# Both pieces of a common slot and all transposes of an ordinary slot at one place between the products, scatters made independent, routing constants issued later

## The chip, the core and the metric

The kernel runs on one core of a Trainium2 chip. The metric is the device time of one execution in microseconds (us); the median of the runs shown is what counts. The engines are PE (TensorE, matrix products and transposes; its weight loads are listed as PEld), DVE (VectorE), ACT (ScalarE), POOL (GpSimd) and SP (SyncE, which only issues transfers). PE's clock has two levels in this case, 2.4 GHz (granted clock 1.00) and 1.2 GHz (0.50).

## The reference, cut to what matters

```python
# attention: B, H, S, D = 4, 8, 576, 64
scores = where(causal, -1e9, q @ k.T / sqrt(D))
local = softmax(scores) @ v
q_p = where(q > 0, q, exp(q) - 1) + 1
mem_out = (q_p @ M_prev) / (q_p @ z_prev + 1e-6)
x = sigmoid(beta) * mem_out + (1 - sigmoid(beta)) * local   # 2304 rows of 512
# mixture of experts: E = 8, F = 1024, one expert a row
logits = x @ w_gate
e_idx = argmax(logits); gate_w = softmax(logits)[e_idx]
eom = sigmoid(x @ w_output_gate)
for e in range(8):
    h = maximum(x[e_idx == e] @ w1[e], 0)
    out[e_idx == e] = gate_w * eom[:, e] * (h @ w2[e])
```

Which expert takes which row is known only at run time. Inputs and result are float32.

## The kernel before

The first part, to about 220 us, is attention. Its instructions stand in an order written out by hand: the string `ORDER` (L50 to L108) names jobs, and each is recorded when its name comes up. Letters tell the kind: `SS` scores on PE, `M` mask and row maximum on DVE, `E` the exponential on ACT, `T` transposes on PE, `V` copies of them out of PSUM, `P` products with v, `C` and `R` the split of q and k into a high part (ACT or DVE) and a low part (POOL, `lo` at L460), `F0` to `F2` the feature map, `TS` small copies of sums on POOL. Before the first job `constants()` (L193) is recorded: three loads and sixteen small POOL instructions that make the tables for the routing (`upper`, `pidx`, `sidx`, `edesc`, `cnt`, `less`, `back`, `tokv`). They are first read by the rank and routing jobs (`RK`, `RT`), which stand far down the string. Right behind them POOL has the last low part of the first tile (L472, `first_low`).

The second part is the mixture of experts. The rows are put into 17 ordinary slots of 128 rows (`NMAIN`), each for one expert. A slot `s` goes through `gather` (POOL, an indirect transfer of its rows), `stage_x` (four transposes on PE into `px`, L1376; two copies on ACT; the low part `xl` on POOL), `gemm1` (first product, 24 matrix products of 512 columns into `h`, L1405, then a rectifier on ACT, L1418), `stage_h` (eight transposes into `hp`, L1431; four copies on ACT; two low parts on POOL), `gemm2` (second product, 24 more into `py`, L1405; scaled on ACT, L1443) and `scatter` (POOL, an indirect transfer to the result). Operands are split into a high and a low part, three terms to a product.

Left-over rows of several experts share common slots: four quarters of 32 rows, then two halves of 64. The weights of such a slot come in 24 transfers of 1 MB (`wide_load`, issued by ACT, four or two instructions each) into two buffers used in turn, and each transfer is used up by one piece on PE (`unit`, L1586): for the quarters four column groups of 32 side by side, for the halves two of 64. Two pieces belong to each ordinary slot from 2 to 13 (`plan[s, 0]`, `plan[s, 1]`), sixteen of quarters in slots 2 to 9 and eight of halves in slots 10 to 13. `refill` issues the load for the buffer that a piece has just freed. A piece waits for its transfer by a semaphore (`T.wait_ge`, L1568).

In the loop (L1640) PE's program for slot `s` is, in this order: `gemm1` of slot s+1 (in four slots with the transposes of a common slot in its middle), the transposes of `stage_x` for slot s+2, the first piece, the first half of `gemm2` of slot s, the transposes of `stage_h` for slot s+1, the second half of `gemm2`, the second piece. The middle comes from the argument `mid`:

```python
i = point(s, 0)
refill(s, 0)
gemm2(s, lambda: (group_rows() if s == 0 else None, stage_h(s + 1)))
i = point(s, 1) or i
refill(s, 1)
```

The scatters all write the tensor `out`. Only those of the last two slots are told to be independent (group `"rows"`); each of the others waits until the one before has landed.

Of the kernel before, what the change touches and what calls it, by code (L numbers as in the profile page):

```python
# [23 lines left out]
NT = B * S  # L24
# [10 lines left out]
NMAIN = 17  # L35
# [20 lines left out]
C3:DVE F12 P1_0_0 E2_1_0 V1_4_1:DVE T2_0 load4 E1_3_0 E1_3_1 V2_0:DVE SS2_2 R3 M2_2_0 M2_2_1 O0_256:ACT O1_0:ACT SS2_3 T2_1 T1_3_1 load_v3 E2_2_0  # L56
V2_1:ACT M2_3_0 V1_3_1:ACT TS1_0 E2_3_0 SS2_4 T1_3_0 V1_3_0:ACT M2_3_1 MW1 F13 F04 E2_2_1 T2_2_0 T2_3_0 TS1_1 M2_4_0 P1_256_0 C4:DVE E2_3_1 F22 MC1
V2_2_0:ACT SS3_1 M3_0_0 V2_3_0:ACT P1_256_1 T2_2_1 M3_1_0 M2_4_1 E2_4 V2_2_1:ACT E3_0_0 load5 F23 O1_256:DVE M3_0_1 T2_3_1 TS2_0 load6 E3_0_1 E3_1_0
# [74 lines left out]
def attn_moe(ctx: ExitStack, tc: tile.TileContext, qk, vd, mz, mt, rz, beta, wgo, w1, w2, out):  # L133
# [59 lines left out]
    def constants():  # L193
        SY.dma_start(gt, beta.partition_broadcast(P))
        SY.dma_start(wg, wgo)
        SY.dma_start(rzt, rz)
        G.affine_select(upper, ones, pattern=[[1, P]], compare_op=ALU.is_gt, fill=0.0, base=0, channel_multiplier=-1)
        G.iota(pidx, pattern=[[1, P]], base=0, channel_multiplier=0, allow_small_or_imprecise_dtypes=True)
# [777 lines left out]
    job("gates", "ACT", 300, 2.0, gates, start=3300)  # L976
    job("gates2", "POOL", 200, 2.0, gates2, after=["gates"])
    job("wgz", "POOL", 300, 6.0, lambda: G.tensor_copy(wgz.rearrange("p n (j c) -> p n j c", j=2), rzt.rearrange("p n (j c) -> p n j c", j=2)[..., D:]) and None, start=4500)
    for g in range(NG):
# [50 lines left out]
    def star_out():  # L1030
        V.scalar_tensor_tensor(jc, stars, 65536.0, jc, op0=ALU.mult, op1=ALU.add)
# [325 lines left out]
    def star_y():  # L1357
        ze["y"] = mk.tile([P, F], F32, name="ye", tag="hl")[:, :DM]
        A.activation(ze["y"], ze["py"], AF.Copy, scale=st["e"]["g"])

    def star_out():
        y = ze.pop("y")
        G.indirect_dma_start(out=out, out_offset=bass.IndirectOffsetOnAxis(ap=rowe, axis=0), in_=y, in_offset=None, bounds_check=NT - 1, oob_is_err=False)

# [55 lines left out]

    def stage_h(s):
        h32 = st[s]["h"]
        hp = pa.tile([P, F], F32, name=f"hp{s}", tag="hp")
        hT = bq.tile([P, F], F32, name=f"hT{s}", tag="hT")
        if s == NMAIN - 1:
            own = cp.tile([P, 2, F], F32R, name="own", tag="w0")
            hh, hl = own[:, 0], own[:, 1]
        else:
            hh, hl = (mk.tile([P, F], F32R, name=f"h{n}{s}", tag=f"h{n}") for n in "hl")
        for f in range(8):  # L1430
            T.transpose(hp[:, f * P:(f + 1) * P], h32[:, f * P:(f + 1) * P], ident)  # L1431
        for n in range(2):
            z = slice(n * 512, (n + 1) * 512)
            A.copy(hT[:, z], hp[:, z])  # L1434
            A.copy(hh[:, z], hp[:, z])  # L1435
            G.tensor_tensor(hl[:, z], hT[:, z], f32(hh)[:, z], op=ALU.subtract)  # L1436
        st[s]["x2"] = hh, hl
# [8 lines left out]
    def finish(s):  # L1446
        for n in range(2):
# [4 lines left out]
            i = G.indirect_dma_start(out=out.rearrange("t (a d) -> (t a) d", a=2), out_offset=bass.IndirectOffsetOnAxis(ap=endi[:, n:n + 1], axis=0), in_=y, in_offset=None, bounds_check=2 * NT - 1, oob_is_err=False)  # L1452
            tc.add_to_no_dep_group("rows", i.ins)
            tc.declare_no_dep(i.ins, group="rows", reason="each slot and half writes its own part of the rows")
        done(s, sem_2)
        st.pop(s)

    def scatter(s):
        i = G.indirect_dma_start(out=out, out_offset=bass.IndirectOffsetOnAxis(ap=outi[:, s:s + 1] if s < NMAIN else fin["outf"][:, s - NMAIN:s - NMAIN + 1], axis=0), in_=st.pop(s)["y"], in_offset=None, bounds_check=NT - 1, oob_is_err=False)
        if s == NMAIN - 2:  # L1460
            tc.add_to_no_dep_group("rows", i.ins)

# [139 lines left out]
    def group_out_rows(kind):  # L1602
        y = mk.tile([P, DM], F32, name=f"yc{kind}", tag="y", bufs=2)
        A.activation(y, cst[kind, "y"], AF.Copy, scale=cst[kind, "g"])
        G.indirect_dma_start(out=out, out_offset=bass.IndirectOffsetOnAxis(ap=group_out[:, kind:kind + 1], axis=0), in_=y, in_offset=None, bounds_check=NT - 1, oob_is_err=False)

    loads = [(0, part, k) for part in range(2) for k in range(8)] + [(1, part, k) for part in range(2) for k in range(4)]
    plan = {}
# [3 lines left out]
    plan[3, "mid"] = lambda: group_turn(0)  # L1612
    plan[5, 1].append(lambda: group_relu(0))
    plan[7, "mid"] = lambda: group_h(0)
    plan[9, 1].append(lambda: group_out_rows(0))
    plan[11, "mid"] = lambda: group_turn(1)
    plan[11, 1].append(lambda: group_relu(1))
    plan[13, "mid"] = lambda: group_h(1)
# [21 lines left out]
    for s in range(NMAIN):  # L1640
        if 0 < s < NMAIN - 1:
            gemm1(s + 1, plan.get((s + 1, "mid")))
        if s + 2 < NMAIN:
            stage_x(s + 2)
            regs(s + 2)
        if s == 1:
            scatter(0)
# [5 lines left out]
        if s == NMAIN - 1:  # L1653
            finish(s)
            break
        i = point(s, 0)
        refill(s, 0)
        gemm2(s, lambda: (group_rows() if s == 0 else None, stage_h(s + 1)))
        i = point(s, 1) or i
        refill(s, 1)  # L1660
        if s == 13:
# [121 lines left out]
```

## Time and profile before

| | |
|---|---|
| runs shown | 478.33, 479.43 and 479.53 us, median 479.43 us |
| profiled execution | 479.24 us, of which the span of instructions is 477.4 us |
| PE | 465.1 us busy, 97% of the span |
| DVE, ACT, POOL | 283.8 us (59%), 262.6 us (55%), 266.0 us (56%) |
| transfers | 80.09 MB, 168 GB/s over the span |
| chain of work that ended last | 91% PE, 3% DVE, 2% POOL, 2% issue |

The profile is one execution. A busy engine is not one at its peak: PE counts as busy while a product drains, so what a change of kind costs it is seen from the starts of its instructions, one after the other, and not from its busy time.

### The profile page before, as it was taken

What the parts mean: (1) busy time and instruction counts of PE and PEld (TensorE: products, weight loads), DVE (VectorE), ACT (ScalarE), POOL (GpSimd) and SP (SyncE); (2) the same over time, 40 slices, a digit from 0 to 9 for tenths busy, and PEclk for the clock granted to TensorE, in tenths of its full rate; (3) what the DMA queues carried; (4) which work ended last, traced back from release to release, by engine and by line L of the source; (5) the groups of instructions that cost most, each with busy time, mean ns of one, the idle gap of its engine ahead of it and who ended that gap; (6) DMA issues with size and microseconds to landing.
All of it is one profiled execution on the core that took longest, in us unless ns stands there. A gap on an engine that the chain in (4) does not pass through costs nothing.

```text
span 477.4 us, 10482 instructions
## 1 busy us (share of the span) xinstructions
PE 465.1 (97%) x3315; PEld 347.9 (73%) x3315; DVE 283.8 (59%) x847; ACT 262.6 (55%) x621; POOL 266.0 (56%) x264
## 2 busy tenths in 40 slices
PE   7999999999999999998999999999999999999994
PEld 4877887877877787746787767767677676676884
DVE  4879898989889987888989807007089500000000
ACT  5889888888878776444543242352423422424241
POOL 8746584555734762453579664536448753443452
PEclk8999999999999999999999999999999999999998
DMA  7544065324131262243298979848699755450101
GB/s 236 186 152 139 23 206 176 136 80 171 56 123 49 85 182 103 67 154 90 66 386 291 336 268 302 288 159 263 224 319 321 273 160 185 141 185 30 36 22 40
DMA packets 34215, 80.09 MB, mean 168 GB/s; under 512 B 4820, under 2 KB 5352, under 8 KB 34154
## 3 DMA queue, kind: packets, MB, share of 16 engines
q1 hardware_dynamic: 17610, 44.05, 27.3%
q10 hardware_dynamic: 12688, 25.30, 15.6%
q0 software_dynamic: 3856, 9.98, 5.9%
q8 instruction: 32, 0.52, 0.5%
q14 instruction: 29, 0.24, 0.2%
HBM read 69.86 MB, written 9.97 MB: 167 GB/s over the span
## 4 chain that ended last, share of the span: by engine, by line
PE 91%; DVE 3%; POOL 2%; issue 2%; POOLq 0%; ACT 0%; DVEq 0%; ACTq 0%
PE h L1405 20%; PE py L1405 18%; PE po L675 10%; PE pt L640 8%; PE s L565 7%; PE me L731 4%; PE cy L1586 3%; PE ch L1586 3%; PE hp L1431 3%; PE sd L552 3%; PE pt L609 2%; PE px L1376 2%; PE pv L794 1%; PE pl L899 1%; PE pye L1130 1%
## 5 line engine op out<-in xcount | busy, mean ns | idle before, releaser
L1436 POOL TENSOR_TENSOR hl<-hT,hh 128x512 fp32r<-128x512 f32 x32 | 46.5, 1472 | 54.5 <-ACT hh L1435 54.5
L628 ACT ACTIVATE st<-st,nm 128x128 f32<-128x128 f32 (+3 forms) x128 | 71.4, 562 | 4.7 <-DVE nm L623 4.6
L1098 DVE CAST whi<-kept 128x1024 fp32r<-128x1024 f32 x32 | 30.0, 938 | 59.4 <-ACTq L1412 50.8
L623 DVE CUSTOM_DVE_ANT_0 st<-s,mask 128x128 f32<-128x128 f32 (+3 forms) x128 | 58.3, 483 | 9.7 <-PE s L565 5.6
L1405 PE MATMUL h<-whi,xh 128*128 (+1 forms) x136 | 55.8, 410 | 0.0
L460 POOL TENSOR_TENSOR lo<-qk,hi 128x1216 fp32r<-128x1216 f32 x15 | 42.1, 2808 | 24.4 <-ACT hi L456 19.0
L487 ACT COPY PT<-pt 128x512 f32<-128x512 f32 (+2 forms) x89 | 45.3, 523 | 15.9 <-PE pt L640 13.8
L1405 PE MATMUL h<-wlo,xh 128*128 (+1 forms) x136 | 53.2, 391 | 0.0
L1405 PE MATMUL h<-whi,xl 128*128 (+1 forms) x136 | 53.1, 391 | 0.0
L1405 PE MATMUL py<-whi,hh 128*128 (+1 forms) x128 | 53.0, 414 | 0.0
L1405 PE MATMUL py<-wlo,hh 128*128 (+1 forms) x128 | 50.2, 392 | 0.0
L1405 PE MATMUL py<-whi,hl 128*128 (+1 forms) x128 | 50.0, 391 | 0.0
L1101 DVE TENSOR_TENSOR wlo<-kept,whi 128x1024 fp32r<-128x1024 f32 x32 | 49.2, 1537 | 1.1
L675 PE MATMUL po<-PT,v 128*64 128x320 f32 (+4 forms) x480 | 49.1, 349 | 0.8 <-ACT oT_hT L487 0.4
L1418 ACT ACTIVATE h<-h 128x1024 f32<-128x1024 f32 x17 | 17.4, 1025 | 57.1 <-PE h L1405 57.1
L640 PE MATMUL pt<-ident,st 128*128 128x128 f32 x320 | 48.3, 282 | 0.0
L1434 ACT COPY hT<-hp 128x512 f32<-128x512 f32 x34 | 20.1, 591 | 49.6 <-PE hp L1431 49.6
L675 PEld LDWEIGHTS po<-PT,v 128*64 128x64 f32 x480 | 29.6, 137 | 17.7 <-issue 2.8
L1384 POOL TENSOR_TENSOR xl<-x,xh 128x512 fp32r<-128x512 f32 x17 | 23.0, 1356 | 32.7 <-ACT x L1383 31.2
L640 PEld LDWEIGHTS pt<-ident,st 128*128 128x128 f32 x320 | 35.8, 143 | 7.0 <-ACT PT L487 1.8
L1435 ACT CAST hh<-hp 128x512 fp32r<-128x512 f32 x32 | 19.1, 596 | 32.3 <-PE py L1405 32.3
L1405 PEld LDWEIGHTS h<-whi,xh 128*128 128x128 f32 x136 | 25.5, 188 | 15.2 <-ACT hh L1435 10.0
(337 smaller groups left out, 1026.3 us busy)
## 6 DMA issues: line engine op xcount, KB each, us to landing
kept<-in_w SPq DMA_DIRECT2D x32, 512.0 KB, 5.3
wide<-in_w ACTq DMA_DIRECT2D x64, 256.0 KB
qk<-in_qk SPq DMA_DIRECT2D x15, 640.0 KB, 4.6
wide<-in_w ACTq DMA_DIRECT2D x16, 512.0 KB
v<-in_vd SPq DMA_DIRECT2D x16, 320.0 KB, 4.3
xs<-xd SPq DMA_DIRECT2D x12, 256.0 KB, 2.2
star<-in_w SPq DMA_DIRECT2D x6, 512.0 KB, 5.2
mz<-in_mz SPq DMA_DIRECT2D x4, 324.0 KB
```

What stands on the lines that cost most here:

```text
L460: G.tensor_tensor(c["lo"][:, TQ:], c["raw"][:, TQ:], f32(c["hi"])[:, TQ:], op=ALU.subtract)
L487: (A.copy if e == "ACT" else V.tensor_copy)(dst(), src())
L565: T.matmul(c()["ss", q][j], l[r, lc], m[r, KC:KC + w], start=(a == 0), stop=(a == 2))
L623: V.tensor_tensor_reduce(st[:, :w], c()["ss", qt][j], mask[:, 512 - w:512], -SCALE, 3.0e38, ALU.add, ALU.min, negm()[:, i:i + 1])
L628: A.activation(st, st, AF.Exp, bias=c()["negm"][:, i:i + 1], scale=-1.0, accum_out=sums()[:, qt, 2 * p + j:2 * p + j + 1])
L640: T.transpose(pt[:, (m * k1 + i) * P:(m * k1 + i + 1) * P], st[:, i * P:(i + 1) * P], ident)
L675: T.matmul(po[64 * j:64 * j + 64, qs - q0:q1 - q0], vt[:, k, 64 * j:64 * j + 64], PT[:, j, k, qs:q1], start=(k == 0), stop=(k == kn - 1))
L1098: join((A.copy if eng is A else eng.tensor_copy)(whi[:, e % 2, c, :], raws[e, c]))
L1101: join(eng.tensor_tensor(wlo[:, e % 2, c, :], raws.pop((e, c)), f32(whi[:, e % 2, c, :]), op=ALU.subtract))
L1405: i = T.matmul(o[n % nh], l[:, z], m[:, n * 512 + part.start:n * 512 + part.stop], start=(c == 0 and k == 0 and n < nh), stop=(c == 3 and ...
L1436: G.tensor_tensor(hl[:, z], hT[:, z], f32(hh)[:, z], op=ALU.subtract)
L1586: i = apart(T.matmul(o[r], x[:, c * P + w * g:c * P + w * g + w], wt[:, g, z], start=first, stop=last, tile_position=(0, w * g)))
```

## The change

Five edits. In slots 2 to 13 (`paired`) both pieces are recorded one behind the other, right after `gemm1` of the next slot; the transposes of `stage_x` and those of `stage_h` follow them together, and `gemm2` runs through without a middle. The rectifier of a common slot (`group_relu`) moves from behind the second piece to behind the transposes of `stage_h` (`turned`). The first `refill` is now issued before the copies of `stage_x`, the second one after them and before the copies of `stage_h`. All scatters of the second part are declared independent of each other. The sixteen POOL instructions of the constants become a job `ranks` that stands behind `TS1_1` in `ORDER`.

```diff
-V2_1:ACT M2_3_0 V1_3_1:ACT TS1_0 ... T2_3_0 TS1_1 M2_4_0 P1_256_0 C4:DVE E2_3_1 F22 MC1
+V2_1:ACT M2_3_0 V1_3_1:ACT TS1_0 ... T2_3_0 TS1_1 ranks M2_4_0 P1_256_0 C4:DVE E2_3_1 F22 MC1
...
+    def ranking_constants():
         G.affine_select(upper, ones, pattern=[[1, P]], ...)
...
+    job("ranks", "POOL", 4000, 8.0, ranking_constants)
...
+    def own_rows(i):
+        tc.add_to_no_dep_group("rows", i.ins)
+        tc.declare_no_dep(i.ins, group="rows", reason="each slot, half and group writes its own rows or parts of them")
...
-    def stage_h(s):
+    def stage_h(s, turned=None):
...
             T.transpose(hp[:, f * P:(f + 1) * P], h32[:, f * P:(f + 1) * P], ident)
+        if turned:
+            turned()
...
     def scatter(s):
         i = G.indirect_dma_start(out=out, ...)
-        if s == NMAIN - 2:
-            tc.add_to_no_dep_group("rows", i.ins)
+        own_rows(i)
...
-    plan[5, 1].append(lambda: group_relu(0))
+    plan[5, "relu"] = lambda: group_relu(0)
...
-    plan[11, 1].append(lambda: group_relu(1))
+    plan[11, "relu"] = lambda: group_relu(1)
...
             gemm1(s + 1, plan.get((s + 1, "mid")))
+        paired = (s, 0) in plan
+        if paired:
+            i = point(s, 0)
+            refill(s, 0)
+            i = point(s, 1) or i
         if s + 2 < NMAIN:
             stage_x(s + 2)
             regs(s + 2)
+        if paired:
+            refill(s, 1)
+            stage_h(s + 1, plan.get((s, "relu")))
...
-        i = point(s, 0)
-        refill(s, 0)
-        gemm2(s, lambda: (group_rows() if s == 0 else None, stage_h(s + 1)))
-        i = point(s, 1) or i
-        refill(s, 1)
+        gemm2(s, None if paired else lambda: (group_rows() if s == 0 else None, stage_h(s + 1)))
```

What this does to PE's row of instructions is seen in slot 5 (`TENSOR_LOAD`, `REGISTER_ALU` and `ISA` set registers for the slots to come). On PE before, between the first product of slot 6 (`h`) and the second product of slot 5 (`py`), stood the transposes of slot 7's rows (`px`) and the first piece (`ch_0`):

```order
L1405 MATMUL h_4775<-wlo,xh_4677 128x512
L1376 MATMUL px_4806<-ident,xr_4636 128x128 x4
L1388 TENSOR_LOAD need
L1388 ISA x2
L1389 TENSOR_LOAD pari
L1389 ISA x2
L1586 MATMUL ch_0_4379<-wide_3964,cx 32x512 x4
L1400 REGISTER_ALU
L1405 ISA
L1405 MATMUL py_4846<-whi,hh_4730 128x512
```

The eight transposes of slot 6 (`hp`) parted the second product, and the second piece (`ch_1`) stood between its end and the first product of slot 7:

```order
L1405 MATMUL py_4846<-wlo,hh_4730 128x512
L1586 MATMUL ch_1_4380<-wide_4036,cx 32x512 x4
L1400 REGISTER_ALU
L1405 ISA
L1405 MATMUL h_4912<-whi,xh_4811 128x512
```

On PE after, both pieces, the four transposes and the eight stand in a row between the first product of slot 6 and the undivided second product of slot 5:

```order
L1413 MATMUL h_4775<-wlo,xh_4691 128x512
L1594 MATMUL ch_0_4348<-wide_3964,cx 32x512 x4
L1594 MATMUL ch_1_4349<-wide_4036,cx 32x512 x4
L1384 MATMUL px_4820<-ident,xr_4636 128x128 x4
L1396 TENSOR_LOAD need
L1396 ISA x2
L1397 TENSOR_LOAD pari
L1397 ISA x2
L1439 MATMUL hp_4853<-ident,h_6_4803 128x128 x8
L1408 REGISTER_ALU
L1413 ISA
L1413 MATMUL py_4876<-whi,hh_4721 128x512
```

So three visits to other work in a slot have become one, and the transposes of `hp` now come that much sooner behind the rectifier that makes their input.

On ACT after, in the same slot, the transfers that refill the first buffer (`wide_3964`) stand between the rectifier of slot 6 (`h_6`) and the copies of slot 7's rows (`xh`, `x_7`), which before came ahead of them:

```order
L1426 ACTIVATE h_6_4803<-h_4775 128x1024
L1542 ISA
L1542 DMA wide_3964<-in_w 128x512
L1542 ISA
L1542 DMA wide_3964<-in_w 128x512
L1542 ISA
L1542 DMA wide_3964<-in_w 128x512
L1542 ISA
L1542 DMA wide_3964<-in_w 128x512
L1389 CAST xh_4825<-px_4820 128x512
L1391 COPY x_7_4828<-px_4820 128x512
L1542 ISA
```

The refill of the second buffer begins with the last of these rows, ahead of the copies of `hp` and not behind the scaling of `py` as before.

On POOL before, at the start of the program, the sixteen constants stood between the clearing of a mask (`maskd`) and the first tile's last low part (`lo_183`); these are their last rows:

```order
L208 MEMSET back 128x9
L210 IOTA tokv 128x20
L212 TENSOR_SCALAR t_204<-tokv 128x20
L213 TENSOR_TENSOR tokv<-tokv,t_204 128x20
L214 MEMSET tokv 64x4
L472 TENSOR_TENSOR lo_183<-qk_157,hi_182 128x320
```

On POOL after, they stand further down, between two copies of sums (`sums`); these are their last rows there:

```order
L210 MEMSET back 128x9
L212 IOTA tokv 128x20
L214 TENSOR_SCALAR t_613<-tokv 128x20
L215 TENSOR_TENSOR tokv<-tokv,t_613 128x20
L216 MEMSET tokv 64x4
L528 COPY sums_219<-sumd_663 64x1
L728 MEMSET lg_692 128x80
L462 TENSOR_TENSOR lo_625<-qk_518,hi_624 128x1216
```

The low part of the first tile has moved up to right behind the masks, and a low part of the fifth pair of heads (`lo_625`) has come to stand behind the constants.

## Rows read from the trace of the kernel before

**Rows 1.** The page, busy time: us (share of the span) x instructions.

```profile
PE 465.1 (97%) x3315; PEld 347.9 (73%) x3315; DVE 283.8 (59%) x847; ACT 262.6 (55%) x621; POOL 266.0 (56%) x264
```

**Rows 2.** Timeline of PE, one slot with pieces: start, us, instruction, count.

```profile
299.31 0.50 PE L1405 MATMUL h<-whi,xh 128*128 x1
299.64 0.39 PE L1405 MATMUL h<-whi,xl 128*128 x1
...
304.89 0.60 PE L1376 MATMUL px<-ident,xr 128*128 128x128 f32 x4
305.42 1.06 PE L1586 MATMUL ch<-wide,cx 128*32 128x512 f32 x8
306.41 0.50 PE L1405 MATMUL py<-whi,hh 128*128 x1
...
309.28 1.04 PE L1431 MATMUL hp<-ident,h 128*128 128x128 f32 x8
310.07 0.48 PE L1405 MATMUL py<-whi,hh 128*128 x1
...
312.68 0.39 PE L1405 MATMUL py<-wlo,hh 128*128 x1
313.00 1.06 PE L1586 MATMUL ch<-wide,cx 128*32 128x512 f32 x8
313.99 0.50 PE L1405 MATMUL h<-whi,xh 128*128 x1
```

**Rows 3.** Timeline of PE, the slot without pieces.

```profile
242.65 0.39 PE L1405 MATMUL h<-whi,xh 128*128 x1
...
248.09 0.60 PE L1376 MATMUL px<-ident,xr 128*128 128x128 f32 x4
...
252.09 0.48 PE L1405 MATMUL py<-whi,hh 128*128 x1
...
254.93 0.39 PE L1405 MATMUL h<-whi,xh 128*128 x1
```

**Rows 4.** Timeline of PE, a piece of halves and what follows it.

```profile
380.21 1.94 PE L1586 MATMUL ch<-wide,cx 128*64 128x512 f32 x8
382.08 0.50 PE L1405 MATMUL py<-whi,hh 128*128 x1
```

**Rows 5.** Timeline of ACT in the slot of Rows 2; ACTq issues transfers.

```profile
305.15 1.02 ACT L1418 ACTIVATE h<-h 128x1024 f32<-128x1024 f32 x1 [4.52 <-PE h L1405]
...
306.82 0.59 ACT L1383 COPY x<-px 128x512 f32<-128x512 f32 x1
307.03 1.35 ACTq L1534 DMA_DIRECT2D wide<-in_w  x3
```

**Rows 6.** Timeline of the start; in brackets idle time before it and its releaser.

```profile
3.79 0.29 POOL L197 TENSOR_SCALAR_AFFINE_SELECT upper<-ones 128x128 bf16<-128x128 bf16 x1
...
4.87 0.35 DVE L467 CAST hi<-qk 128x320 fp32r<-128x320 f32 x1
...
7.41 0.86 POOL L472 TENSOR_TENSOR lo<-qk,hi 128x320 fp32r<-128x320 f32 x1
...
8.33 0.50 PE L565 MATMUL s<-lo,hi 64*128 64x512 f32 x2 [1.49 <-POOL lo L472]
...
13.27 0.61 ACT L628 ACTIVATE st<-st,nm 128x384 f32<-128x384 f32 x1 [0.87 <-DVE nm L623]
```

**Rows 7.** Busy time by stretch, then granted clock (PEclk), DMA share, GB/s.

```profile
8.90:12.20 3.30, 3.30 (x18) 2.76 (x15) 1.92 (x6) 3.27 (x8) 3.13 (x2) 0.50 1.05 411
...
12.30:470.00 457.70, 454.34 (x3265) 341.33 (x3265) 278.42 (x828) 254.81 (x603) 254.70 (x230) 1.00 0.49 168
...
255.00:374.00 119.00, 119.00 (x623) 85.31 (x622) 60.85 (x49) 42.64 (x72) 69.65 (x52) 1.00 0.81 277
```

**Rows 8.** Timeline of POOL where the constants are put.

```profile
31.95 0.18 POOL L526 COPY sums<-sumd 64x1 f32<-64x1 f32 x1
36.52 0.18 POOL L526 COPY sums<-sumd 64x1 f32<-64x1 f32 x1 [4.39 <-ACT st L600]
```

**Rows 9.** Waits of POOL: us in total, times, longest.

```profile
POOL out L1459 <- DMA out<-yc,group_out: 2.2, 2, 1.9
```

More of the change, by code (lines that the diff above doesn't have):

```diff
@@ L56 @@
 C3:DVE F12 P1_0_0 E2_1_0 V1_4_1:DVE T2_0 load4 E1_3_0 E1_3_1 V2_0:DVE SS2_2 R3 M2_2_0 M2_2_1 O0_256:ACT O1_0:ACT SS2_3 T2_1 T1_3_1 load_v3 E2_2_0
-V2_1:ACT M2_3_0 V1_3_1:ACT TS1_0 E2_3_0 SS2_4 T1_3_0 V1_3_0:ACT M2_3_1 MW1 F13 F04 E2_2_1 T2_2_0 T2_3_0 TS1_1 M2_4_0 P1_256_0 C4:DVE E2_3_1 F22 MC1
+V2_1:ACT M2_3_0 V1_3_1:ACT TS1_0 E2_3_0 SS2_4 T1_3_0 V1_3_0:ACT M2_3_1 MW1 F13 F04 E2_2_1 T2_2_0 T2_3_0 TS1_1 ranks M2_4_0 P1_256_0 C4:DVE E2_3_1 F22 MC1
 V2_2_0:ACT SS3_1 M3_0_0 V2_3_0:ACT P1_256_1 T2_2_1 M3_1_0 M2_4_1 E2_4 V2_2_1:ACT E3_0_0 load5 F23 O1_256:DVE M3_0_1 T2_3_1 TS2_0 load6 E3_0_1 E3_1_0
@@ L1359, in star_y @@
         A.activation(ze["y"], ze["py"], AF.Copy, scale=st["e"]["g"])
+    def own_rows(i):
+        tc.add_to_no_dep_group("rows", i.ins)
+        tc.declare_no_dep(i.ins, group="rows", reason="each slot, half and group writes its own rows or parts of them")
     def star_out():
         y = ze.pop("y")
-        G.indirect_dma_start(out=out, out_offset=bass.IndirectOffsetOnAxis(ap=rowe, axis=0), in_=y, in_offset=None, bounds_check=NT - 1, oob_is_err=False)
+        i = G.indirect_dma_start(out=out, out_offset=bass.IndirectOffsetOnAxis(ap=rowe, axis=0), in_=y, in_offset=None, bounds_check=NT - 1, oob_is_err=False)
+        own_rows(i)
     def gather(s, gate=True):
@@ L1452, in finish @@
             i = G.indirect_dma_start(out=out.rearrange("t (a d) -> (t a) d", a=2), out_offset=bass.IndirectOffsetOnAxis(ap=endi[:, n:n + 1], axis=0), in_=y, in_offset=None, bounds_check=2 * NT - 1, oob_is_err=False)
-            tc.add_to_no_dep_group("rows", i.ins)
-            tc.declare_no_dep(i.ins, group="rows", reason="each slot and half writes its own part of the rows")
+            own_rows(i)
         done(s, sem_2)
@@ L1459, in scatter @@
         i = G.indirect_dma_start(out=out, out_offset=bass.IndirectOffsetOnAxis(ap=outi[:, s:s + 1] if s < NMAIN else fin["outf"][:, s - NMAIN:s - NMAIN + 1], axis=0), in_=st.pop(s)["y"], in_offset=None, bounds_check=NT - 1, oob_is_err=False)
-        if s == NMAIN - 2:
-            tc.add_to_no_dep_group("rows", i.ins)
+        own_rows(i)
     def split(e, c, eng):
@@ L1604, in group_out_rows @@
         A.activation(y, cst[kind, "y"], AF.Copy, scale=cst[kind, "g"])
-        G.indirect_dma_start(out=out, out_offset=bass.IndirectOffsetOnAxis(ap=group_out[:, kind:kind + 1], axis=0), in_=y, in_offset=None, bounds_check=NT - 1, oob_is_err=False)
+        i = G.indirect_dma_start(out=out, out_offset=bass.IndirectOffsetOnAxis(ap=group_out[:, kind:kind + 1], axis=0), in_=y, in_offset=None, bounds_check=NT - 1, oob_is_err=False)
+        own_rows(i)
     loads = [(0, part, k) for part in range(2) for k in range(8)] + [(1, part, k) for part in range(2) for k in range(4)]
```

## The prediction

> **What bounds the kernel now.** I read the page first: PE is busy 97% of the span, every other engine under 60% [rows 1]. Such a share could hide slack, since a product counts as busy while it drains. So the second view is the timeline of PE alone in the second part, start by start. In a slot with pieces products follow each other every 0.23 us (23 starts from 299.64 to 304.89), and nothing there waits for another engine: the only longer steps are those where the kind of work changes [rows 2]. The busy time of the stretch from 255 to 374 us says the same, 119.00 of 119.00 us at a granted clock of 1.00 [rows 7]. The second part is thus as long as PE's row of instructions, and what shortens that row shortens the kernel. The third view is the start, since one edit is there: PE stands idle 1.49 us before 8.33 us, and POOL's low part `lo` ended that wait [rows 6]. The profiled execution took 479.24 us, 0.2 below the median; I count from it.
>
> **The price of a change of kind.** From 299.31 to 313.99 us a slot with pieces takes 14.68 us; the slot without takes 12.28 us (242.65 to 254.93) [rows 2, 3]. Two pieces and their switches thus cost 2.40 us. A piece of quarters lasts 0.99 us to the next start, one of halves with twice the passes 1.87 us [rows 2, 4], so two passes cost 0.88 us, and the four passes of two pieces 1.76 us. The other 0.64 us are switches: before a piece the last product takes 0.32 us (312.68 to 313.00) and not 0.23; behind a piece 0.11 us are left over beside its passes; and the first product after it needs 0.33 us (299.31 to 299.64) until the next. That makes about 0.3 us for one visit, twice a slot. The change leaves one visit.
>
> **The pieces and transposes, term by term.** A slot after the change, from the start of `gemm1` to the next, is the sum of four terms.
> - First product: 24 in a row took 5.44 us (242.65 to 248.09) [rows 3], with no restart since it follows a product. Its last now stands before a piece: plus 0.09. 5.53 us.
> - Two pieces: four passes, the form that one piece of halves has already, 1.87 us to the next start [rows 4].
> - Twelve transposes: eight take 0.79 us (309.28 to 310.07) [rows 2]. That is 7 steps of 0.11 and a last short one, so four more add 0.44 us. Starting behind a piece may cost up to the 0.10 us that a product pays there; I take 0.05. 1.28 us.
> - Second product undivided: twelve behind transposes took 2.84 us (252.09 to 254.93, the restart in it) and twelve more at the pace of the first product take 2.72 [rows 3]. 5.56 us.
>
> Together 14.24 us, 0.44 less than 14.68. For the pieces of halves the same terms stand with four passes more on both sides, so the saving is the same. Twelve slots give 5.3 us. Joining the two groups of transposes is worth nothing by itself: one restart behind them goes, about 0.09 us, and the short last step of one group goes with it, 0.08 us.
>
> **The bounds of that term.** The trace of before never shows one piece right behind another with its own buffer and its own semaphore. Nearest below is the inside of a piece of halves, where the weights of the later passes load under the earlier ones: the 1.87 us. Nearest above is two lone pieces, 2 x 0.99 = 1.98 us. I take the first, because the last passes of a piece of halves also read new weights. The end above costs 0.11 us a slot, 1.3 us in all; a full 0.10 for the start of the transposes 0.6 us more. On the good side 0.50 us a slot is possible if the products keep the pace of 24 in a row throughout and the transposes start free. So 3.4 to 6.0 us, and I take 5.3.
>
> The Trainium skill, "TensorE: Matmul & The Clock Gate", Part 3 (packing small matmuls), says that a weight load overlaps matmuls in flight only where its row group differs or it goes to the background buffer. The pieces share all rows and differ in columns; read strictly, the second would load behind the first, 2 x 0.99, and the sum would end 1.3 us higher. Rows 4 stand against that reading.
>
> **What the moved steps now wait for.** The transposes `hp` read the rectifier's output. It starts 0.26 us after the start of `px` and takes 1.02 us (305.15) [rows 5], so it ends 1.28 us after the point where the pieces will now begin, give or take 0.1. The pieces and four transposes put about 2.3 us before `hp`. That is 1 us of cover; were it gone, each slot would pay what is missing. ACT then issues the first refill before the copies of `px`: three issues took 1.35 us [rows 5], four about 1.8. The copies (0.59 each) and POOL's low part behind them are wanted only by the next `gemm1`, a whole second product (5.56 us) after the transposes. From the first piece that is 1.87 + 1.28 + 5.56 = 8.7 us, and by 1.3 + 1.8 + 1.1 + 1.3 (POOL) + 0.5 of latency they are done at about 6. Second refill, copies of `hp` and two low parts come behind that on ACT and POOL; their consumer is the second product of the next slot, some 8 us later still. POOL's gate transfers move behind `hl` and are read only when `py` is scaled. None of it should reach PE.
>
> **Transfers.** The second buffer is now refilled some 3 us after the first and not 7, and both are wanted again together. The second is issued some 4 to 5 us into the block of small work and used 15.1 us into it (14.24 + 0.88), which leaves 10 us; both together, 2 MB, have about 13. From 255 to 374 us the rate was 277 GB/s [rows 7], so a slot of 14.68 us moves 4.1 MB; in 14.24 us that is 286 GB/s, and the start of the program moved 411 GB/s [rows 7]. So there is room, but not in every order: if other queues take more than half while both refills are under way, the second piece waits.
>
> **Scatters.** The wait that the edit removes is one of POOL's, 2.2 us in two places [rows 9], on an engine with 44% idle, before a low part that PE wants much later. I count 0. At the end only the last transfer's landing counts, which was independent before.
>
> **Start.** POOL spends the time from 3.79 us to 7.41 on the constants and then 0.86 us on `lo`, though its input was there when DVE's cast ended at 5.22 us [rows 6]. Moved, `lo` ends at about 6.1 us and PE goes on where it stopped, at 6.84. So PE gains at most 1.49 us. ACT limits it: its first idle time behind the start is 0.87 us before 13.27 [rows 6], so it comes at most 0.87 us earlier there, and PE's next transposes need what it makes. Between 0.87 and 1.49 I take 1.0, since every later job follows its producers with little cover and the engines move together. The constants fall into a hole of 4.39 us on POOL, before 36.52 [rows 8], and need at most 3.62: free, with 0.8 us to spare. From below the term may vanish or turn negative, by the clock (third rival).
>
> **Sum.** 479.24 - 5.3 - 1.0 = **472.9 us**, nothing for the rest.
>
> **Rivals.**
> - The second piece does not load under the first. Against it speaks the inside of the piece of halves; for it, that the buffers and the semaphore differ. 1.3 us less gain: 474.2 us.
> - The second refill lands late. Priced at 1.2 us a slot in the eight slots of quarters, where 1 MB a buffer meets the experts' loads (277 GB/s), that is +9.6 us: 482.5 us, **slower than before**. It decides from 0.8 us a slot (6.3 / 8). For it: both refills now queue together. Against: the stretch has shown no wait at 277 GB/s, and 13 us for 2 MB asks 160 GB/s of a rate that has reached 411.
> - The half clock moves. The granted clock was 0.50 from 8.9 to 12.2 us [rows 7], after PE had stood idle from 6.84 to 8.33. There ACT set the pace, so it cost little. With that idle time gone PE is ahead of ACT and may idle about 1.3 us somewhat later, around 10 to 12 us; if the clock then falls in the stretch behind, where PE's work is dense, 3.3 us at half clock lose up to 1.65 us. The start then gives -0.65 instead of 1.0: 474.6 us.
> - The clock falls in each slot, since 3.1 us of small work now stand in one place. A half-clock stretch as long as that of rows 7 would lose 1.65 us in each of 12 slots: 479.24 - 6.3 + 19.8 = 492.7 us, a loss from the fourth slot on (6.3 / 1.65 = 3.8). Against it: from 12.3 to 470 us the clock stayed at 1.00 [rows 7], through pieces of 1.87 us and through all of attention with its transposes. The Trainium skill, same page, Part 4 (PE-mode transpose), holds that transposes do not count as PE activity for the clock; by that this rival would be likely. The trace of attention does not bear it out.
> - The change does nothing for the time: what the switches give is lost waiting for the rectifier, 1 us of cover gone in every slot. 478.5 to 479.5 us.
>
> **How the numbers follow.** Forecast 472.9 us: 0.68. Weights not hidden, 474.2: 0.11. Half clock at the start moved, 474.6: 0.10. Late refill, 482.5: 0.05, of which a mild form (under 0.6 us a slot) still ends faster: 0.02. Clock in each slot, 492.7: 0.03. Nothing: 0.03. The best corner is 479.24 - 6.0 - 1.5 = 471.7; the first three cases with the bounds 3.4 and -0.65 reach 476.5 only if both misses fall together, so I cut at 475.4. With some 0.4 us between runs the range is 471.2 to 475.4. About 0.3%, 1.4 us, is what a measurement can tell from no change. Faster: 0.68 + 0.11 + 0.10 + 0.02 = 0.91; within: 0.03; slower: 0.06.
>
> **What would show it.** In the timeline of PE after, a quarter slot should start its `gemm1` 14.2 us after the last one, the two pieces 0.85 to 0.9 us apart, `px` 1.8 to 1.9 us behind the first of them, and no idle time before `hp`. If `px` comes 2.0 behind, the weights were not hidden. A wait of the second piece shows as a start more than 1 us behind the first. In the first 16 us PE's scores should run on at 6.8, and the second part should begin about 1 us earlier than 220 us. POOL should show the sixteen constants before 36 us. I am wrong in the main if slots stay at 14.6 us, or if a wait of PE for ACT or a transfer stands in front of `hp` or the second piece.

## The result: slower, 1.009 of the time before

The kernel after takes 483.14 us (median of 12 runs, 480.5 to 486.2), beside 479.31 us for the kernel before on the same chip (12 runs, 478.3 to 481.9). The ratio is 1.0091, with a 95% interval of 1.0072 to 1.0111. The forecast was 472.9 us with a range of 471.2 to 475.4: the sign is wrong. The profiled execution of after took 484.48 us, with a span of 482.7; that of before 479.24.

The page of after, lines that answer to [rows 1] and the chain of work that ended last:

```profile
PE 464.0 (96%) x3315; PEld 349.9 (72%) x3315; DVE 282.9 (59%) x847; ACT 262.1 (54%) x621; POOL 265.1 (55%) x264
...
PE 82%; DMA 7%; DVE 4%; issue 2%; ACT 1%; ACTq 1%; POOL 1%; POOLq 0%; DVEq 0%
PE h L1413 16%; PE py L1413 14%; PE po L677 9%; PE pt L642 8%; DMA wide<-in_w 7%; PE s L567 7%; PE me L733 4%; PE hp L1439 3%; PE cy L1594 3%; PE ch L1594 3%; PE sd L554 3%; PE px L1384 2%; PE pt L611 2%; PE pv L796 1%; PE pl L901 1%
```

PE is still the busiest engine. What is new is a transfer in the chain: `wide<-in_w`, the refill of a piece's buffer, with 7% of the span (the chain counts a late transfer from its issue on, so this is more than PE's idle time). The waits of PE in after (us in total, times, longest) name the place:

```profile
PE ch L1594 <- DMA wide<-in_w: 3.9, 2, 3.3
PE cy L1594 <- DMA wide<-in_w: 3.3, 1, 3.3
```

Three waits in all, each for the second piece of a common slot. First a slot without a wait, which answers to [rows 2]; timeline of PE in after (start, us, instruction, count):

```profile
289.25 1.92 PE L1594 MATMUL ch<-wide,cx 128*32 128x512 f32 x16
291.11 0.66 PE L1384 MATMUL px<-ident,xr 128*128 128x128 f32 x4
291.60 1.04 PE L1439 MATMUL hp<-ident,h 128*128 128x128 f32 x8
...
297.96 0.39 PE L1413 MATMUL h<-whi,xh 128*128 x1
```

The two pieces stand in one row (x16) of 1.86 us to the next start, the transposes take 0.49 and 0.79 us, and the first product of the next slot starts at 297.96. It had started at 283.72 in this slot, so the slot is 14.24 us, where [rows 2] show 14.68. That is the prediction's number to the hundredth. The slot that follows:

```profile
303.49 1.07 PE L1594 MATMUL ch<-wide,cx 128*32 128x512 f32 x8
307.85 1.94 PE L1594 MATMUL ch<-wide,cx 128*32 128x512 f32 x8 [3.29 <-DMA wide<-in_w]
309.71 1.12 PE L1384 MATMUL px<-ident,xr 128*128 128x128 f32 x4
310.62 1.91 PE L1439 MATMUL hp<-ident,h 128*128 128x128 f32 x8
312.19 0.78 PE L1413 MATMUL py<-whi,hh 128*128 x1
```

The second piece starts 4.36 us behind the first and not 0.88; in brackets is the idle time and its releaser. What comes behind is slower as well: the second piece takes 1.86 us to the next start, `px` 0.91 and `hp` 1.57, about twice the times above. The window behind the wait, beside the answer to the last line of [rows 7] (length, busy us, then granted clock, share of the transfer engines, GB/s), shows why:

```profile
306.50:313.50 7.00, 5.65 (x23) 3.80 (x24) 0.00 (x0) 1.51 (x3) 1.27 (x1) 0.51 0.66 236
...
255.00:374.00 119.00, 111.81 (x581) 80.99 (x580) 56.91 (x46) 38.93 (x66) 63.81 (x49) 0.96 0.76 260
```

PE stood idle for 3.29 us, and behind that the granted clock is 0.51, the 1.2 GHz of its two levels. The other two late second pieces:

```profile
275.75 1.06 PE L1594 MATMUL ch<-wide,cx 128*32 128x512 f32 x8 [0.58 <-DMA wide<-in_w]
...
371.89 1.94 PE L1594 MATMUL cy<-wide,cx 128*32 128x512 f32 x8 [3.33 <-DMA wide<-in_w]
```

The sum closes. Against 14.24 us the excess of the three slots is 0.91, 6.13 and 4.94 us (second pieces at 275.75, 307.85 and 371.89). Of these 12.0 us, 7.75 are the later starts of the second pieces (0.76 + 3.48 + 3.51) and 4.2 are the slower work behind them. 484.48 - 12.0 = 472.5 us: by this sum the kernel after would have met the forecast without the three waits. It is the sum of one profiled execution, 1.3 us above the median of runs that spread over 5.7 us.

### The profile page after: what moved, and what is told of

It is laid out like the page before. It is cut to its first block, busy times and chain, and to the rows that moved or that the text cites. A ratio compares the mean times of both kernels' runs of the same rounds, so it can differ in the third digit from the quotient of the medians.

```text
span 482.7 us, 10478 instructions
## 1 busy us (share of the span) xinstructions
PE 464.0 (96%) x3315; PEld 349.9 (72%) x3315; DVE 282.9 (59%) x847; ACT 262.1 (54%) x621; POOL 265.1 (55%) x264
## 4 chain that ended last, share of the span: by engine, by line
PE 82%; DMA 7%; DVE 4%; issue 2%; ACT 1%; ACTq 1%; POOL 1%; POOLq 0%; DVEq 0%
PE h L1413 16%; PE py L1413 14%; PE po L677 9%; PE pt L642 8%; DMA wide<-in_w 7%; PE s L567 7%; PE me L733 4%; PE hp L1439 3%; PE cy L1594 3%; PE ch L1594 3%; PE sd L554 3%; PE px L1384 2%; PE pt L611 2%; PE pv L796 1%; PE pl L901 1%
## 5 line engine op out<-in xcount | busy, mean ns | idle before, releaser
L1101 DVE CAST whi<-kept 128x1024 fp32r<-128x1024 f32 x32 | 31.4, 982 | 67.7 <-issue 32.1
L1413 PE MATMUL h<-whi,xh 128*128 (+1 forms) x136 | 54.3, 399 | 0.0
L1413 PE MATMUL py<-whi,hh 128*128 (+1 forms) x128 | 51.9, 406 | 0.0
L1104 DVE TENSOR_TENSOR wlo<-kept,whi 128x1024 fp32r<-128x1024 f32 x32 | 47.0, 1468 | 1.1
L1375 POOL DMA_INDIRECT xr<-xs,rowi x17 | 19.7, 1161 | 18.5 <-issue 11.0
```

What stands on the lines that cost most here:

```text
L1101: join((A.copy if eng is A else eng.tensor_copy)(whi[:, e % 2, c, :], raws[e, c]))
L1104: join(eng.tensor_tensor(wlo[:, e % 2, c, :], raws.pop((e, c)), f32(whi[:, e % 2, c, :]), op=ALU.subtract))
L1413: i = T.matmul(o[n % nh], l[:, z], m[:, n * 512 + part.start:n * 512 + part.stop], start=(c == 0 and k == 0 and n < nh), stop=(c == 3 and ...
```

## What the transfer engines had to do

The chain of waits of after follows the second piece of 307.85 back to its refill on ACT's queue (start, us, what):

```profile
292.86 0.37 ACTq L1540
...
294.83 12.97 DMA wide<-in_w
307.80 0.04 issue
307.85 1.94 PE ch L1594 x8
```

The refill's issue begins at 292.86, and the last of its four transfers is on its way for 12.97 us. Two rows of the timelines of SP and ACT say what was asked for shortly before:

```profile
289.12 7.88 SPq L390 DMA_DIRECT2D kept<-in_w  x4
```

```profile
290.68 1.91 ACTq L1540 DMA_DIRECT2D wide<-in_w  x4
```

These are four loads of an expert's weights (512 KB each, into the buffers `kept`) and the first refill. The views of the transfers from 288 to 308 us show how full the engines were, with the busy share in 40 slices; first before, with a window of that stretch, then after:

```profile
DMA  9978999899959999999999999956477948998998
...
DMA packets 2540, 6.08 MB, mean 304 GB/s; under 512 B 343, under 2 KB 343, under 8 KB 2538
```

```profile
290.00:302.00 12.00, 12.00 (x66) 8.27 (x65) 5.68 (x5) 4.84 (x8) 6.86 (x7) 1.00 0.97 333
```

```profile
DMA  0000949766589999899999999999999869969799
...
DMA packets 2296, 5.62 MB, mean 281 GB/s; under 512 B 331, under 2 KB 331, under 8 KB 2294
```

In before as in after the engines are nearly full there: from 290 to 302 us before shows a share of 0.97 at 333 GB/s. Until the late piece began, this slot of after had the four expert loads (2.10 MB), 1.04 MB of gathers and scatters and both refills (eight transfers of 256 KB, 2.1 MB) under way: 5.2 MB. The first refill was issued at 290.68 and the second piece wanted at 303.49 + 0.88 = 304.37, 13.7 us later; at 333 GB/s the 5.2 MB need an estimated 15.6 us. The Trainium skill, "DMA: Bandwidth & Descriptors", Specifications, gives some 358 GB/s as a core's limit for HBM; by that the 5.2 MB would need an estimated 14.5 us. The start of the program moves 411 GB/s [rows 7], above that figure, so it stands here as the page's and not as a limit that the rows show. Both estimates are coarse, since half of the gathers and scatters ran only after 304.37. The view of just these 13.7 us of after (290.68 to 304.37; queue, packets, MB, share; q10 is ACT's queue with the pieces, q1 SP's with the expert weights, q0 POOL's gathers and scatters) says what was missing:

```profile
DMA packets 1762, 4.44 MB, mean 324 GB/s; under 512 B 222, under 2 KB 222, under 8 KB 1760
...
q10 hardware_dynamic: 1032, 1.89, 44.7%
q1 hardware_dynamic: 552, 2.00, 37.7%
q0 software_dynamic: 176, 0.52, 10.3%
```

Other queues took more than half of the 4.44 MB, and 0.2 MB of the 2.1 MB of refills were not there in time. These 0.2 MB took 3.4 us more, while the other queues went on as well: from 304.37 to 307.80 us they moved 1.00 MB, half of it gathers and scatters, and part of the rest the next first refill, issued at 304.92. But a burst doesn't make a wait by itself. A fourth slot with a burst, from 326.21 to 340.0 us, moved 4.39 MB at 319 GB/s, only 0.23 MB of them by POOL; both refills were complete in time, and nothing waits.

In before the same bytes were moved. There the second refill was issued from 300.87 and wanted at 313.00 us, 12.1 us later; in after these are 292.86 and 304.37, 11.5 us. So it has about as much time as before. But before it ran when the burst was mostly over (busy share 0.84 from 302 to 308 us and 0.49 from there to 314), and now it falls into the burst together with the first refill.

That is an argument. The experiments tell it from two others: that the second refill is asked for too late, behind the copies of `px` on ACT; and that two refills at once are too much for the queue by themselves.

## Experiments

Each ratio is to the kernel before, run beside the variant. The median of before was 478.5 to 479.3 us from chip to chip, so differences in us between two variants can be off by that much.

### Without the expert loads

```diff
-        send(raw, fetching["e"], c)
+        if e < 2:
+            send(raw, fetching["e"], c)
```

> The kernel after, with the transfers of the weights of the experts from the third on left out (the splits run on what lies in the buffers, so the products of these experts are not those of the reference). First theory, that the second piece of a slot waits because its refill is in flight together with the other refill and with a burst of expert weights: the three waits (about 9.5 us in all) and the half clock behind them (about 2.3 us) go, and the time is 472 to 474 us. Second theory, that the second refill is asked for too late because it stands behind the copies of px on ScalarE: issues stand where they stood, so waits of 3 to 4 us stay in the same slots, 480 us or more. Third theory, that two refills of a slot are too much for the transfer engines by themselves: waits stay in many slots, 480 us or more.

Measured 475.03 us, ratio 0.9919 (0.9898 to 0.994). No wait of PE for a transfer is left and no half clock behind one. Window and first wait of PE:

```profile
255.00:374.00 119.00, 117.32 (x630) 87.45 (x629) 63.32 (x50) 43.19 (x73) 69.90 (x54) 1.00 0.55 182
```

```profile
PE h L1414 <- POOL xl L1393: 1.7, 1, 1.7
```

The share of the transfer engines is 0.55 where after has 0.76, and the clock 1.00. The third theory falls: two refills at once are no trouble when they have the engines to themselves. So does the second, since the order of the issues on ACT is unchanged. The time is 1 us above the expectation because of the wait in the second fence, which I hadn't counted: at 369 us POOL had four transfers of its own to issue (a group's gather, a slot's gather and two scatters) before the low part `xl`. After itself doesn't have this wait.

### The second refill issued right behind the first

```diff
             refill(s, 0)
             i = point(s, 1) or i
+            refill(s, 1)
 ...
-            refill(s, 1)
             stage_h(s + 1, plan.get((s, "relu")))
```

> The kernel after, with the second refill of a slot issued right behind the first, ahead of ScalarE's copies of px instead of behind them. Both issues stand about 2 us nearer to each other. Second theory (issue too late): the waits of about 4 us shrink by the 2 us that the issue comes earlier and the slack of 0.04 us elsewhere becomes 2 us, time 475 to 478 us. First theory (rate of the transfer engines while a burst of expert weights is under way): the second transfer starts earlier but its end is set by all bytes asked for by then, so the waits keep most of their length: gain 0 to 2 us, 481 to 484 us.

Measured 483.17 us, ratio 1.0066 (1.0039 to 1.0093). Weight loads of PE that waited, and the eight issues on ACT in the slot from 291 us:

```profile
PEld ch L1594 <- DMA wide<-in_w: 6.2, 2, 4.1
PEld cy L1594 <- DMA wide<-in_w: 3.0, 1, 3.0
```

```profile
291.17 5.00 ACTq L1540 DMA_DIRECT2D wide<-in_w  x8
```

The waits keep most of their length (9.2 us; in after the same rows say 5.7 and 4.6, 10.3). But the second refill was hardly asked for earlier. The first six of the eight issues follow each other every half microsecond, and the fifth, with which the second refill begins, is this one:

```profile
293.25 0.34 ACTq L1540 DMA_DIRECT2D wide<-in_w  x1
```

That is 2.08 us behind the first issue (291.17); in after it is 2.18 (290.68 to 292.86), and the last issue of the eight stands 4.63 us behind the first, in after 4.15. So the copies of `px` had held the second refill up by only 0.1 us, and the 2 us that the expectation counts on weren't there to win. The second theory is out here too, since what it blames costs next to nothing; what asking 2 us earlier would bring isn't shown by this run. The copies now stand behind eight issues, and PE waits 1.3 us for the low part `xl`, which it doesn't in after.

### Expert weights through two buffers in place of four

```diff
-        raw = raws[e, c] = kept[n % 4]
+        raw = raws[e, c] = kept[n % (2 if e > 1 else 4)]
```

> The kernel after, with the weights of the experts from the third on going through two of the four 512 KB buffers, so that at most 1 MB of them is in flight at a time instead of 2 MB; all bytes are still moved. First theory: a burst leaves the refills more of the transfer engines, the waits for second pieces shrink or go, 473 to 479 us, unless the expert's weights themselves then come late (a wait of the first product of a slot for a split would show it). Second and third theory: no change, 482 to 485 us.

Measured 475.35 us, ratio 0.9917 (0.9885 to 0.995). The same bytes, at most 1 MB of expert weights in flight. The waits of PE:

```profile
PE ch L1594 <- DMA wide<-in_w: 2.0, 1, 2.0
```

One wait of 2.0 us is left of three, in the slot of 302.50, and no product waits for an expert's weights. 7.8 us less than after, with the same bytes, come from a burst that is smaller and spread out: the four loads that SP issues within 7.88 us from 289.12 in after take 32.54 us from 293.83 here. The first theory holds.

### The same ring in the kernel before

The same line, in the kernel before.

> The kernel before with the weights of the experts from the third on going through two of the four buffers, as in the runs with the ring of two and the third buffer. In the kernel before PE waits for no piece, so the smaller bursts have nothing to give: a ratio of 1.000, 0.5 us either way. If the ring of two were itself what made the run with the third buffer fast, 2 us or more would go here.

Measured 479.46 us, ratio 1.0009 (0.9993 to 1.0026). Before has no late piece, so the smaller burst gives nothing. So the gain of the other run comes from the waits of after.

### A third buffer

```diff
-        b = u % 2
+        b = u % 3
 ...
+        elif b not in wide:
+            wide[b] = kept[2:4]
 ...
-        raw = raws[e, c] = kept[n % 4]
+        raw = raws[e, c] = kept[n % (2 if e > 1 else 4)]
 ...
-    ahead = [2]
+    ahead = [3]
 ...
+        if s == 1:
+            wide_load(2)
```

Not shown are the lines that index three buffers in place of two, and one that reads a group's expert numbers a slot earlier.

> The kernel after with a third 1 MB buffer for pieces, made of two of the four expert buffers (so the expert weights from the third on go through two, as in the run with two). Each transfer of a piece is asked for one piece earlier, so has about a slot and a half instead of a slot. First theory: no PE wait for a piece is left, the clock stays at 1.00, and the time is what the sum of the prediction gave, 472 to 474 us. If a second cause holds the late pieces (the waits are not for transfers, or the half clock comes from the slot's order and not from the waits), it stays above 478 us.

Measured 476.42 us (475.6 to 479.1), ratio 0.9962 (0.9943 to 0.9981): 6.7 us less than after, but 2.4 above the end of the expectation. No piece waits for its transfer. My own edit put a wait elsewhere; the profile is of the slowest run, 479.10 us. Timeline of ACT, wait of PE, and the window behind it:

```profile
259.98 2.95 ACTq L1546 DMA_DIRECT2D kept<-in_w  x4
262.98 0.59 ACT L1577 COPY cx<-pc 128x512 f32<-128x512 f32 x1 [6.73 <-DVE wlo L1104]
```

```profile
PE ch L1599 <- ACT cx L1577: 3.7, 1, 3.7
```

```profile
263.50:269.50 6.00, 5.88 (x29) 2.90 (x30) 3.84 (x4) 2.06 (x4) 0.00 (x0) 0.55 0.78 226
```

ACT's issue into the new buffer waits for DVE, which is still splitting the weights that lie there, and the copy `cx` that PE needs stands behind it on ACT. PE idles 3.70 us, and the clock falls to 0.55 behind it, as in after, this time without any late transfer. So the half clock can follow a stall of PE whatever the cause of the stall.

### The third buffer, first filled a slot later

```diff
-    ahead = [3]
+    ahead = [2]
 ...
             refill(s, 1)
+            if s == 2:
+                refill(s, 1)
 ...
-        if s == 1:
-            wide_load(2)
```

The edit is against the run above.

> The run with a third buffer had no wait for a piece, but one of 4.1 us of PE at 259.6 us for ScalarE's copy cx, which stood behind the first issue into the new buffer, and the half clock behind it (2.5 us). Here that issue moves from the slot before into the first slot with pieces, behind the pieces. If these two places were all that was left, the profiled time is 472 to 473.5 us, with the clock at 1.00 and slots of 14.24 us. If the extra transfers asked for in that slot make the next pieces late, one wait of 1 to 4 us stands at the second slot, 474 to 478 us.

Measured 472.68 us (472.4 to 473.4), ratio 0.9857 (0.9827 to 0.9888). This is the forecast's time, and it beats both kernels. Chain and window:

```profile
PE 91%; DVE 4%; issue 2%; ACT 1%; POOL 1%; POOLq 0%; DVEq 0%; ACTq 0%
```

```profile
255.00:374.00 119.00, 119.00 (x640) 89.19 (x639) 47.30 (x43) 42.71 (x72) 69.58 (x54) 1.00 0.79 275
```

No transfer is left in the chain, PE is busy in 119.00 of 119.00 us at clock 1.00, with the engines at 275 GB/s, nearly the average of [rows 7]. So the mean rate was not what made after slow. This run has two remedies, the smaller burst (475.35 us by itself) and the buffer that lets each transfer be asked for a piece earlier, some 2.7 us more on another chip.

### The second piece back behind the second product

```diff
-            i = point(s, 1) or i
 ...
-            refill(s, 1)
-            stage_h(s + 1, plan.get((s, "relu")))
+            stage_h(s + 1)
 ...
+        if paired:
+            i = point(s, 1) or i
+            refill(s, 1)
+            if (s, "relu") in plan:
+                plan[s, "relu"]()
```

> The kernel after with the second piece of a slot and its refill behind the undivided second product, so the two pieces are apart as before, while all transposes stay together. If the loss of after comes from wanting both pieces together, there is no wait for a transfer here and the clock stays at 1.00. By the prediction's prices the start gives 1.0 us and the joined transposes about 0.17 us a slot, 2 us in 12 slots: 475.5 to 477.5 us. If the joined transposes were what costs, it is slower than before, above 480 us.

Measured 478.51 us, ratio 0.9991 (0.9971 to 1.0011), 1 us above the expectation. No piece waits. Timeline of PE, the refill on ACT and its transfers (KB each, median us from issue to landing):

```profile
303.50 1.07 PE L1594 MATMUL ch<-wide,cx 128*32 128x512 f32 x8
...
311.43 1.06 PE L1594 MATMUL ch<-wide,cx 128*32 128x512 f32 x8
```

```profile
299.39 3.17 ACTq L1540 DMA_DIRECT2D wide<-in_w  x4
```

```profile
wide<-in_w ACTq DMA_DIRECT2D x4, 256.0 KB, 4.0
```

The refill that after asks for at 292.86 is asked for here at 299.39, and its four transfers land 4.0 us after their issues, where the last one of after took 12.97. Asked for 6.5 us later, behind the burst (which SP issues from 287.54 to 294.14 us here), it comes no later; it is wanted at 311.43 and is there. A slot is 14.59 us, from the first piece at 288.91 to the one at 303.50. So the joined transposes are worth 0.09 us a slot, and I had expected 0.17; that is 1 us less gain in twelve slots. The rest is mine: I put the group's rectifier behind the refill's issues, and `chp` waits for it (479.25 - 1.0 - 12 x 0.09 + 1.4, the wait and a slower start behind it, is 478.6):

```profile
PE chp L1605 <- ACT ch L1600: 1.1, 1, 1.1
```

### The pieces together, the transposes apart

```diff
-            stage_h(s + 1, plan.get((s, "relu")))
 ...
-        gemm2(s, None if paired else lambda: (group_rows() if s == 0 else None, stage_h(s + 1)))
+        gemm2(s, lambda: (group_rows() if s == 0 else None, stage_h(s + 1, plan.get((s, "relu")))))
```

> The kernel after with the transposes hp back in the middle of the second product: the pieces together, the transposes apart. If the loss comes from wanting both pieces together, the same three waits (9 to 10 us in all) and the half clock behind them stay: 481 to 485 us. If the joined transposes or their order on ScalarE hold the transfers up, the waits go and the time is below 477 us.

Measured 480.14 us, ratio 1.003 (1.0006 to 1.0054), below what I expected. Waits of PE, and two windows behind them:

```profile
PE ch L1594 <- DMA wide<-in_w: 2.8, 2, 1.7
PE cy L1594 <- DMA wide<-in_w: 2.6, 1, 2.6
```

```profile
303.00:314.00 11.00, 9.09 (x52) 5.84 (x52) 0.00 (x0) 3.42 (x6) 3.46 (x4) 1.00 0.91 295
363.00:375.00 12.00, 9.32 (x54) 6.04 (x53) 10.23 (x9) 3.30 (x5) 10.16 (x7) 1.00 0.98 356
```

The waits stand in the same three slots, as expected, but with 5.4 us are shorter than after's 7.2, and the clock stays at 1.00 in both windows, behind the two longest: the slower work of after (4.2 us) mostly goes. Why the waits are shorter by these 2 us I can't say from one profile; runs of this kernel spread over 4 us. The slots without a wait are 14.27 us (289.78 to 304.05), so beside joined pieces the joined transposes are worth 0.03 us a slot.

### Both pieces together in the slots of halves alone

```diff
-        paired = (s, 0) in plan
+        paired = s >= 10 and (s, 0) in plan
 ...
+        if not paired:
+            i = point(s, 0)
+            refill(s, 0)
 ...
+        if not paired:
+            i = point(s, 1) or i
+            refill(s, 1)
+            if (s, "relu") in plan:
+                plan[s, "relu"]()
```

> The kernel after with the slots of quarters (the first eight slots with pieces, where the expert weights still come) in the order of before, and the four slots of halves in the order of after. If both pieces at one place are harmless where no burst of expert weights runs, there is no wait for a piece, and the time is 479.2 less 1.0 for the start less 4 times 0.44: 476 to 477 us. If slots of halves lose too, it is 478 us or more.

Measured 477.57 us, ratio 0.9975 (0.996 to 0.999). No piece waits. It is 0.6 us above the end of the expectation, and again `chp` waits 1.1 us for the rectifier that I put behind the refill (1.4 with the slower start behind it). Without that, 476.2. Where no expert loads come, both pieces at one place make no piece wait, and the time is 0.25% below before's.

### The start alone, the scatters alone

```diff
-... T2_3_0 TS1_1 M2_4_0 ...
+... T2_3_0 TS1_1 ranks M2_4_0 ...
```

> The kernel before with the constants moved alone. The trace of after shows the second part starting 0.97 us earlier and no later wait tied to it: 0.9 to 1.1 us less than before, a ratio of 0.998. If the start's gain is given back somewhere, or the half clock at the start costs more, the ratio is 1.000 or above.

> The kernel before with the scatters' independence alone. It ends POOL waits of 2.2 us in two places on an engine with 44 per cent idle. The prediction counted 0: within 0.3 us of before, a ratio of 1.000. If those waits reached PE through the low parts behind them, 1 to 2 us less.

The start alone: 478.22 us, ratio 0.9977 (0.9958 to 0.9996), 1.0 us less, as expected. The scatters alone (`own_rows` on every scatter): ratio 1.0006 (0.9993 to 1.002), nothing, as expected.

## Why the prediction was wrong

Point by point, by its own steps:

- **The slot.** Right in sum, 14.24 us. Measured, with the predicted value in brackets: first product 5.53 (5.53), two pieces 1.86 (1.87), transposes 1.28 (1.28), second product 5.57 (5.56). The weights of the second piece do load under the first: its start is 0.88 us behind. The reading of the Trainium skill, "TensorE: Matmul & The Clock Gate", Part 3, by which each piece would have cost 0.99, is not what the rows show.
- **The transposes.** "Joining the two groups is worth nothing by itself" was right (0.03 to 0.09 us a slot); the 0.17 that the same sentence works out, and that I used for one experiment, was too much.
- **The rectifier, ACT's and POOL's order, the scatters.** No wait in front of `hp`, no late copy; right.
- **The start.** Right: PE's scores run on, where [rows 6] have the wait of 1.49 us, and the half clock of [rows 7] is gone with it. Rows of after:

```profile
7.61 0.40 PE L567 MATMUL s<-hi 64*128 64x512 f32 x2
8.32 0.78 PE L567 MATMUL s<-lo,hi 64*128 64x384 f32 x2 [0.31 <-DVE nm L625]
```

```profile
8.90:12.20 3.30, 2.88 (x22) 2.09 (x20) 3.03 (x11) 3.30 (x10) 1.41 (x1) 1.00 1.05 413
```

- **The transfers: the step that failed.** The prediction set an average of 286 GB/s a slot against the 411 of the start, and concluded "So there is room". Both sides were wrong. The 277 GB/s are a mean over 119 us with bursts and quiet stretches, and a late piece is made by the slot with the burst: there the engines moved 4.44 MB in 13.7 us, a rate of 324 GB/s. And 411 GB/s is no ceiling that holds for this mix: from 290 to 302 us of before the engines are nearly full at 333. The two refills needed 160 GB/s by the prediction; they got 1.89 MB in 13.7 us, 138 GB/s, and three second pieces waited, 12.0 us in all with the slower work behind them. The share of 0.81 stood in [rows 7] beside the rate, and I read the rate. The prediction did say "if other queues take more than half while both refills are under way, the second piece waits", but looked at no slot to see whether they do. In the slot from 290.68 us of after they took 2.5 of 4.44 MB. The view and the window of before, above, would have shown engines without room.
- **The rival.** The late refill was named, with 482.5 us; 483.14 came. It was given 0.05. Its size is right partly by chance: it was spread as 1.2 us over eight slots, and came as 0.9, 6.1 and 4.9 us in three of the four slots with a burst.
- **The clock.** The rival "the clock falls in each slot" did not come: in slots without a wait, and from 219 to 430 us of the run with the later third buffer, it is 1.00, with 1.3 us of transposes behind 1.86 us of pieces in each. On the Trainium skill's rule that transposes don't count for the clock (same page, Part 4) these rows say only that so many of them in a row did not lower it. But a price was missing in the rival of the late refill: the work behind two long idle times of PE ran at half clock, 4.2 us of the 12.0 lost.

## What to carry to other kernels

When two transfers that were wanted at different times get one deadline, don't ask for the average rate: take the slot with the largest burst, add up the bytes of all queues in it up to the deadline, divide by the rate that the trace shows at a busy share near 1, and compare with the time to the deadline. The sum tells where it is tight and not how late it gets: of two slots that moved 4.4 MB before the deadline, one was 0.2 MB short and waited 3.3 us, and the other had no wait. What helped was a smaller burst from the other queue, and with it a buffer more; whether asking 2 us earlier by itself helps wasn't tried. Of an edit that orders instructions, check what each issue that can wait has behind it on its engine: three of my own experiments lost 1 to 6 us in that way.

## What the runs showed of the hardware

- Nearly full engines don't have one rate. The busy share is 0.97 at 333 GB/s from 290 to 302 us of before, 0.98 at 356 from 363 to 375 us of the run with the transposes apart, and 1.05 at 411 in [rows 7]. Here the share told that there was no room; the rate alone didn't.
- A refill that was 0.2 MB short at its deadline came 3.4 us late, while the other queues went on moving (290.68 to 307.80 us of after).
- Behind idle times of PE of 3.29, 3.33 and 3.70 us in its dense part the granted clock was 0.51, 0.50 (371.8 to 374.8 us of after) and 0.55; behind waits of 2.0 and 2.6 us (the ring of two, the transposes apart) it stayed at 1.00. At the start it was 0.50 behind 1.49 us of idle time [rows 6, rows 7], and 1.00 behind 0.31 us. So the length of the last wait alone doesn't decide it, and what else does wasn't tried.
